# Spectral filter, real 2-D transform and MoE block: how the operands of the first group of slots reach TensorE

## The chip, the cores and the metric

One core of a Trainium2 chip runs the whole kernel. The metric is device time in microseconds (us), the median of several executions of the program. Before the change it is 1440.38 us.

## The reference

```python
def _attn_ref(x, filt_r, filt_i):            # x: 8 x 3136 x 256
    X = np.fft.rfft(x, axis=1)
    F = (filt_r + 1j * filt_i)[None, :, :]
    Y = X * F
    return np.fft.irfft(Y, n=x.shape[1], axis=1).astype(np.float32)

def _moe_ref(x, w_ch1, w_ch2):               # x is the result of _attn_ref
    X = np.fft.fft(x, axis=1)
    X = np.fft.fft(X, axis=2)
    mixed = np.real(X).astype(np.float32)
    u = x + mixed
    mu = np.mean(u, axis=-1, keepdims=True)
    var = np.mean((u - mu) ** 2, axis=-1, keepdims=True)
    un = (u - mu) / np.sqrt(var + 1e-06)
    ch = np.maximum(un @ w_ch1, 0.0) @ w_ch2
    return (u + ch).astype(np.float32)
```

So each batch is filtered in the frequency domain along its 3136 positions, the real part of a 2-D transform of the result is added, and a layer norm with a two-layer network (256 to 1024 to 256) follows, whose output is added to u.

## The kernel before, in words

**Work.** The transform of length 3136 = 56 x 56 is done in two stages of matmuls, forward and back. For each batch: `forward1` makes the first stage (matmul `s`, copies `ast`) and stores it to DRAM (`d1`), `forward2` loads it turned (`at`), makes the second stage, multiplies with the filter (`yt`), folds the spectrum into `ef` and `eo` for the mixing and transposes it to `z`, `inverse1` makes the first inverse stage (matmul `i`, copies `bt`, DRAM `d2`), and `inverse2` loads that (`b`), makes the second (`y`), and stores it slot by slot (`ys`, DRAM `dy`). A slot is a pair of positions (n and 3136 - n), 1568 of them to a batch. The second half works on 49 groups of 256 slots, in two tiles of 128: `mixture` makes the transform along channels from the folded spectrum (matmul `mix`, a row `nyq` for the middle frequency), `add` adds it to y on VectorE (DVE), `moments` and `scales` make the layer norm's numbers, `prepare` makes un, its two float16 halves `u16` and their transpose `ut` (by a transposing DMA), `first_product` makes eight `h` (6 matmuls of 512 columns each; relu on ScalarE (ACT), low half on DVE), `second_product` makes `acc` (96 matmuls of 256 columns a group), which is added to y and stored.

**Group 0** is a case of its own, since it ends the run-up: its y is made by `direct` (L776) for tile 0 and 1 from `b_0` and `b_1`, two loads of 512 KB from the DRAM copy `d_f` that the 14 stores of L699 filled; its mixture is copied (`near` L1001, `point` L1002) and added with eight operations on DVE and four of one row (L924); its `ut` is transposed on TensorE (PE; L313), not by a DMA. `prepare_first` holds this.

**Weights** come as pairs of words, are widened (L1147 to L1154), squared for a bound (L1158), bounded (L1197, L1199, a power of two through a matmul `pb` and L296 to L303) and split in a high and a low half (ACT L1223, DVE L1210): first `w1`, then `w2` between group 0's first products. Tables at L49 to L55 (LOAD_AT, WIDEN_AT, SQUARE_AT, BOUND_AT, SPLIT_AT) say at which step. **Warm** matmuls (L283, `idle`, result unused) stand on PE where it would wait in the run-up: 18 behind `inverse1`, 10 behind the mixture, 4 behind each of six pairs of y.

**Order.** A generator for each batch and the loop over q (group and eighth of it) near L1343 place the work; a scheduler moves instructions within each engine, held by `with after(...)` marks. Group 1 and on need only batch 0 until group 6, the first that needs batch 1. Batch 1's `forward1` starts behind group 0's end, and batch 2's while group 5 runs. Each engine runs its own instructions in order, DMAs of SP (SyncE) too.

Of the kernel before, what the change touches and what calls it, by code (L numbers as in the profile page):

```python
# [49 lines left out]
LOAD_AT = (2, 2, 2, 2, 41, 42, 46, 50)  # L50
LOAD_IN = ("b2", "b2", "ys", "ys", "b2", "b2", "ys", "ys")
WIDEN_AT = (31, 33, 37, 41, 58.3, 58.3, 74, 74)
SQUARE_AT = (44, 46, 58.1, 58.1, 68, 68, 1002, 1002)
BOUND_AT = (58.2, 1003)
# [38 lines left out]
def constants():  # L93
# [83 lines left out]
    cols = np.arange(56)  # L177
    near = np.zeros((112, 2, 128))
    far = np.zeros((112, 2, 256))
    for kind in range(2):  # L180
        s_, q = cols // 28, cols % 28
        near[:, kind, :56] = i2f[0].reshape(112, 112)[:, 56 * s_ + 28 * kind + q]
        far[:, kind, 112:168] = i2f[1].reshape(112, 112)[:, 56 * (s_ if kind == 0 else 1 - s_) + 28 * kind + q]
    direct = np.concatenate([near.reshape(112, 256), far.reshape(112, 512)], 1)
# [16 lines left out]
        "c_y": np.ascontiguousarray(direct).astype(np.float32),  # L201
# [14 lines left out]
def _program(ctx, tc, nc, a, NB):  # L216
# [91 lines left out]
    def flip(dst, src, pool, tag, name, late):  # L308

        m, n, q = src.shape  # L310
        pt = pool.tile([128, 8, 128], F16, tag=tag, name=name)
        for i in range(n):
            nc.tensor.transpose(pt[:q, i, :m], src[:, i], ident16[:m, :m])  # L313
# [16 lines left out]
    def settle():  # L330
# [5 lines left out]
        homes["y16"] = [*y16s, cp.tile([128, 4, 2, 128], F16, name="y16_3")]  # L336

    sxs, alphas, dys, esps = {}, {}, {}, {}

# [9 lines left out]
    def prepare_filters():  # L349
# [4 lines left out]
        pow2(mF[:, 11:12], "F", pF, spare)  # L354
# [12 lines left out]
    def first_forward1():  # L367
# [23 lines left out]
        load_weights(3)  # L391
# [5 lines left out]
        tables["y"] = direct[:112]  # L397
        nc.sync.dma_start(direct, a["c_y"])
# [44 lines left out]
    def forward1(b, d1):  # L443
# [3 lines left out]
        for q in range(7 + XLAG):  # L447
            with after(("y", 1), ("un", 0)) if b == 1 and q > 2 else after(("b", 1)) if b == 1 else nullcontext():
# [3 lines left out]
                k = q - XLAG  # L452
                if k >= 0 and b in SQUARED:
# [55 lines left out]
    def load_halves():  # L509
# [4 lines left out]
        with after("sp"):  # L514
            nc.sync.dma_start(s1, a["c_s1"])
            fill_tails(0, 1)
# [10 lines left out]
    def forward2(b, d1, d2):  # L527
# [25 lines left out]
        def spectrum(ch, hf):  # L553
# [57 lines left out]
            if b == 0:  # L611
# [3 lines left out]
                for j in range(4):  # L615
                    nc.tensor.transpose(pt[:, j], yh[:, :, j].rearrange("p r q -> p (r q)"), ident)
# [16 lines left out]
        def fold_sums(ch):  # L633
            yt = yts[ch]
            pool, tag, bufs = (fp, "ef", 1) if b else (mp, "u16", 2) if ch < 2 else (fp, "x16", 3)
# [19 lines left out]
        def fold_halves(ch):  # L655
# [6 lines left out]
            for r0, e0, n in ((g0, 0, cut), (0, cut, 224 - cut)):  # L662
                if n:
# [6 lines left out]
                    else:  # L670
                        with after("spread", "utt", "w2s", ("cast", 1)):
                            nc.scalar.activation(hi, e, AF.Copy, scale=first)
# [3 lines left out]
        def inverse1(ch, h):  # L676
# [4 lines left out]
            if b == 0:  # L681
# [4 lines left out]
                if j == 26:  # L686
                    idle.append(ps_o.tile([128, 512], F32, tag="pso", name="idle"))
                    warm(18, "i1", ("pb", "F"), p=idle[0])
                marks["spread"] = nc.scalar.copy(bt, p).ins
            else:  # L690
# [7 lines left out]
                nc.vector.tensor_tensor(bt[:, :, 1], p, bt[:, :, 0], op=ALU.subtract)  # L698
            marks["bt", ch] = nc.sync.dma_start(d2[:112, j : j + 2], bt).ins  # L699

        far = 3
        for c in range(far if b else 0):
            load(c)
            yield
        ups = {(0, 0): 1, (0, 1): 2, (1, 0): 3, (1, 1): 4, (3, 0): 5, (4, 0): 6}
# [27 lines left out]
    def inverse2(b, d2):  # L733
# [29 lines left out]
        def direct(t, tile0, tile1):  # L763

            p = bank(f"y0_{t}").rearrange("p (k c) -> p k c", k=2)
            table = tables["y"]
            for k in range(2):
                first, last = (0, 2) if t == 0 else (2, 4)
                for j in range(first, last + 1):
                    if j == 0:  # L770
                        w = table[:, 128 * k : 128 * k + 128]
                    else:
                        o = 256 + 256 * k + 112 - 56 * j + 128 * t
                        w = table[:, o : o + 128]
                    with after("warm"):
                        marks["i2"] = nc.tensor.matmul(  # L776
                            p[:, k], w, (tile0, tile1)[j // 4][:, j % 4], start=j == first, stop=j == last
# [3 lines left out]
        load(0)  # L781
        for c in range(1, 6) if b == 0 else ():
# [3 lines left out]
        for c in range(14):  # L786
            if b == 0 and c < 2:
                direct(c, bts[0], bts[1])
                if c:
                    del bts[0]  # L790
# [43 lines left out]
            with after("warm" if c < 8 else "pe"):  # L834
# [3 lines left out]
            if c < 8:  # L838
                warm(4, "i2", p=idle[0])
            with after("utt"):  # L840
# [51 lines left out]
    def fetch(g):  # L892
        y = ys_of[g] = mp.tile([128, 2, 2, 256], F32, tag="y", name=f"y_{g}", bufs=4)
        for t, (g0, g1) in enumerate(groups[g]):
            q = g0
            while q < g1:
                b = q // NS
                e = min(g1, (b + 1) * NS)
                with after(("un", 0)) if g == 2 else after(("out", g - 4)):
# [46 lines left out]
    def mixture(g):  # L946
# [4 lines left out]
        for t, (g0, g1) in enumerate(tiles):  # L951
            n = g1 - g0
            r0 = g0 % RING
            channels(pm[:n, t], lambda e, h: homes["eo"][:, e, h, r0 : r0 + n], t == 0, t == len(tiles) - 1, g == 1)
# [42 lines left out]
    def prepare_first():  # L997
# [3 lines left out]
        nc.scalar.copy(near, pm)  # L1001
        marks["near"] = nc.scalar.copy(point[:1, 0], fix[0][2]).ins  # L1002
        pm, fix = near, [(t, row, point[:1, 0], a) for t, row, _, a in fix]
        yield
        y = mp.tile([128, 2, 2, 256], F32, tag="y", name="y_0", bufs=4)
        ut = mp.tile([128, 2, 8, 128], F16, tag="ut", name="ut_0", bufs=2)
        mv, st, sb = small(0)
        al = alphas[0]
        for t in range(2):
            add(y[:, t], pm[:, t], al, sums[t])  # L1010
            for tf, row, pn, _ in fix:
                if tf == t:
                    add_nyquist(y[row, t, 1], pn, al[row], sums[t][row, 1])
            moments(0, y, [(t, groups[0][t])], st, mv)
            roots(0, sb, mv, [(128, slice(2 * t, 2 * t + 2))])
            yield
        for t in range(2):
            scales(0, sb, mv, [(128, slice(2 * t, 2 * t + 2))])
            yield
            un = mp.tile([128, 2, 256], F32, tag="un", name=f"un_0_{t}", bufs=2)  # L1020
            u16 = mp.tile([128, 2, 2, 2, 128], F16, tag="u16", name=f"u16_0_{t}", bufs=2)
            unv = un.rearrange("p k (d q) -> p k d q", q=128)
            for k in range(2):
                i = 2 * t + k
                if t and k:
                    nc.vector.tensor_scalar(un[:, k], y[:, t, k], sb[:, i, 3:4], sb[:, i, 1:2], op0=ALU.mult, op1=ALU.add)
                else:
                    nc.scalar.activation(un[:, k], y[:, t, k], AF.Identity, bias=sb[:, i, 1:2], scale=sb[:, i, 3:4])
            marks["cast", 0] = nc.scalar.copy(u16[:, :, :, 0], unv).ins
# [6 lines left out]
    def prepare(g):  # L1036
# [7 lines left out]
        for t, (g0, g1) in enumerate(tiles):  # L1044
            ps = slice(0, g1 - g0)
            with after(("u16", 0)) if g == 1 else after("h", *((("un", 1), "w2l") if g == 2 else ())):
# [36 lines left out]
    def first_product(g, f):  # L1083
# [4 lines left out]
        p = ps_h.tile([128, 512], F32, tag="psh", name=f"h_{g}_{f}")  # L1088
# [52 lines left out]
    def widen(dst, raw, name, late):  # L1141
# [12 lines left out]
        v.scalar_tensor_tensor(dst, size, tiny, dst, op0=ALU.is_ge, op1=ALU.mult)  # L1154
# [7 lines left out]
    def load_weights(i):  # L1162
# [5 lines left out]
        pool, bufs = {"b2": (fp, 2), "ys": (fp, 3)}[LOAD_IN[i]]  # L1168
# [3 lines left out]
    def widen_weights(i):  # L1172
        name = ("w1", "w2")[i // 4]
        if i % 4 == 0:
            raws[name] = [], tp.tile([128, 5], F32, tag="mw", name="m" + name)
# [5 lines left out]
        ws.append(w)  # L1181
        if a[name].dtype == F32:
            nc.sync.dma_start(w, words[i])
        else:
            with after("low", "first" if i > 4 else "", "utc"):
                widen(w, words[i], f"{i}", i > 3)

    def square_weights(i):
        name = ("w1", "w2")[i // 4]
        ws, m = raws[name]  # L1190
        with after("act", "spread" if i > 1 else "", "near" if i > 3 else "", "w1s" if i > 3 else "", "utt", "relu"):
            squares(m[:, i % 4 : i % 4 + 1], ws[i % 4], f"{name}_{i % 4}")

    def bound_weights(name):
# [3 lines left out]
        with after("utt", "relu"):  # L1198
            marks["root"] = nc.scalar.activation(m[:, 4:5], m[:, 4:5], AF.Sqrt, scale=0.25).ins  # L1199
        sw = tp.tile([128, 2], F32, tag="sw", name="s" + name)  # L1200
        pow2(m[:, 4:5], name, sw, spare, "i1" if name == "w1" else "pe")
# [236 lines left out]
```

## Time and profile before

| what | value |
|---|---|
| median of 3 runs | 1440.38 us (1440.06 to 1441.49) |
| the profiled execution | 1439.6 us, span 1437.8 us, mean granted clock 0.996 |
| PE (matmul) busy | 1394.2 us, 97% of the span |
| DVE, ACT, POOL busy | 1048.4 (73%), 755.8 (53%), 508.3 us (35%) |
| HBM read, written | 124.41 MB, 99.17 MB |

The span runs from the first to the last instruction; 1.8 us of the execution lie outside it. TensorE's matmuls take nearly all of it, so the table is read from there: the columns of the other engines matter where TensorE waits for them.

### The profile page before, as it was taken

How to read it: one execution, taken by the hardware profiler on the slowest of the kernel's cores; microseconds unless marked ns; L12 is line 12 of the kernel's file. 1: busy time of each engine (PE TensorE's matmuls, PEld its weight loads, DVE VectorE, ACT ScalarE, POOL GpSimd, SP SyncE). 2: the span in 40 equal slices, each digit the busy share in tenths (PEclk: the TensorE clock that was granted, in tenths of full speed). 3: DMA queues.
4: the chain of work that ended last, by engine and by line, in shares of the span. 5: the costliest groups of instructions: out<-in, count | busy, mean ns of one | idle time of the engine just before them, and what ended most of it. 6: DMA issues, size and time to landing. Idle time of an engine off the chain costs nothing.

```text
span 1437.8 us, 30014 instructions
## 1 busy us (share of the span) xinstructions
PE 1394.2 (97%) x11274; PEld 949.9 (66%) x11274; DVE 1048.4 (73%) x2327; ACT 755.8 (53%) x1422; POOL 508.3 (35%) x641
## 2 busy tenths in 40 slices
PE   9989999989999999999999999999999999999998
PEld 8745775557666776666766676666766667666666
DVE  7786794678688876978578866977779876555553
ACT  6757455546365554745546554655447554434341
POOL 2422591069102940067300870038401673011010
PEclk9999999999999999999999999999999999999999
DMA  9668987798947967589576987489575977453220
GB/s 358 211 210 237 240 182 238 213 209 204 257 137 205 256 159 231 157 220 240 162 229 180 245 182 224 148 222 246 139 258 167 230 179 195 112 157 78 85 60 30
DMA packets 434221, 276.42 MB, mean 192 GB/s; under 512 B 218796, under 2 KB 401084, under 8 KB 434076
## 3 DMA queue, kind: packets, MB, share of 16 engines
q1 hardware_dynamic: 433948, 274.47, 70.2%
q8 instruction: 88, 1.44, 0.4%
q14 instruction: 57, 0.47, 0.1%
q10 hardware_dynamic: 128, 0.05, 0.0%
HBM read 124.41 MB, written 99.17 MB: 155 GB/s over the span
## 4 chain that ended last, share of the span: by engine, by line
PE 63%; DVE 9%; DMA 8%; issue 5%; ACT 5%; POOL 3%; SPq 3%; DVEq 0%; ACTq 0%; POOLq 0%
PE h L1097 25%; PE acc L1127 24%; PE s L495 3%; PE y L812 2%; DMA x<-x 2%; DMA at<-d 2%; PE mix L914 2%; DVE y L924 2%; DVE h L1108 1%; ACT un L1068 1%; POOL u L1072 1%; DMA d<-ast 1%; PE s L592 1%; PE i L694 1%; PE s L593 1%
## 5 line engine op out<-in xcount | busy, mean ns | idle before, releaser
L1097 PE MATMUL h<-ut,home 128*128 128x512 f16 x2352 | 581.5, 380 | 20.9 <-DVE h L1108 12.9
L1127 PE MATMUL acc<-w2s,h 128*128 128x256 f16 x4704 | 598.5, 273 | 3.0 <-DVE y L1136 1.5
L1127 PEld LDWEIGHTS <-h 128*128 128x128 f16 x4704 | 455.1, 98 | 150.6 <-issue 17.8
L1107 ACT ACTIVATE h<-h 128x512 f16<-128x512 f32 x392 | 233.1, 595 | 390.5 <-PE h L1097 385.6
L1108 DVE SCALAR_TENSOR_TENSOR h<-h,h 128x512 f16<-128x512 f32 x392 | 267.9, 684 | 212.5 <-ACT h L1107 210.8
L1097 PEld LDWEIGHTS <-home 128*128 128x128 f16 x2352 | 222.7, 98 | 230.0 <-issue 34.3
L1072 POOL TENSOR_TENSOR u<-un,u 128x512 f16<-128x512 f32 x96 | 111.0, 1172 | 670.9 <-ACT u L1071 618.8
L924 DVE SCALAR_TENSOR_TENSOR y<-mix,alpha,y 128x508 f32<-128x508 f32 (+1 forms) x360 | 152.8, 476 | 1.7 <-PE mix L914 0.6
L1068 ACT ACTIVATE un<-y,sb 128x256 f32<-128x256 f32 x192 | 99.8, 591 | 35.3 <-DVE sb L988 33.2
L609 POOL TENSOR_TENSOR yt<-yt,t 128x224 f32<-128x224 f32 x108 | 73.4, 679 | 115.9 <-DVE t L601 87.8
L698 DVE TENSOR_TENSOR bt<-i,bt 112x512 f16<-112x512 f32 x98 | 66.4, 684 | 32.5 <-ACT bt L697 32.3
L1136 DVE SCALAR_TENSOR_TENSOR y<-acc,beta,y 128x512 f32<-128x512 f32 x98 | 71.5, 744 | 21.6 <-PE acc L1127 21.5
L821 ACT ACTIVATE ys<-y,alpha 128x512 f32<-128x512 f32 x98 | 64.1, 684 | 43.3 <-PE y L812 42.9
L639 POOL TENSOR_TENSOR ef<-yt 128x224 f32<-128x224 f32 x112 | 73.4, 675 | 34.5 <-ACT wsq_w L1158 15.7
L623 POOL TENSOR_TENSOR home<-yt,home 128x448 f16<-128x448 f32 x77 | 79.3, 1035 | 8.8 <-ACT home L622 8.8
L697 ACT CAST bt<-i 112x512 f16<-112x512 f32 x98 | 56.8, 584 | 43.0 <-PE i L696 38.3
L597 DVE SCALAR_TENSOR_TENSOR yt<-s,pF,ft 128x448 f32<-128x448 f32 x98 | 66.0, 675 | 17.4 <-PE s L593 15.5
L610 POOL TENSOR_TENSOR yt<-yt,t 128x224 f32<-128x224 f32 x108 | 74.8, 694 | 0.0
L972 DVE BATCH_NORM_STATS2 st<-y 128x6 f32<-128x256 f32 x196 | 73.1, 411 | 0.2
L306 DVE TENSOR_REDUCE mx<-x 112x1 f32<-112x1024 f32 x42 | 51.0, 1215 | 30.2 <-DMA x<-x 30.0
L601 DVE SCALAR_TENSOR_TENSOR t<-s,pF,ft 128x448 f32<-128x448 f32 x98 | 66.1, 676 | 0.5 <-POOL yt L610 0.5
L669 POOL TENSOR_TENSOR eo<-ef,eo 128x448 f16<-128x448 f32 (+6 forms) x55 | 51.5, 940 | 33.8 <-ACT eo L668 32.3
(173 smaller groups left out, 1660.8 us busy)
## 6 DMA issues: line engine op xcount, KB each, us to landing
x<-x SPq DMA_DIRECT2D x55, 512.0 KB
out<-y SPq DMA_DIRECT2D x98, 256.0 KB
at<-d SPq DMA_DIRECT2D x49, 512.0 KB
b<-d SPq DMA_DIRECT2D x49, 512.0 KB
dy<-ys SPq DMA_DIRECT2D x206, 112.0 KB
y<-dy SPq DMA_DIRECT2D x90, 256.0 KB
d<-ast SPq DMA_DIRECT2D x98, 224.0 KB
d<-bt SPq DMA_DIRECT2D x98, 224.0 KB
```

What stands on the lines that cost most here:

```text
L609: nc.gpsimd.tensor_tensor(yh[:, 0], yh[:, 0], t2v[:, 1], op=ALU.subtract)
L610: marks["sum"] = nc.gpsimd.tensor_tensor(yh[:, 1], yh[:, 1], t2v[:, 0], op=ALU.add).ins
L623: nc.gpsimd.tensor_tensor(ylo, ytv, yhi, op=ALU.subtract)
L639: nc.gpsimd.tensor_tensor(ef[:, i], yt[:, 0, i], yt[:, 1, i], op=o)
L924: nc.vector.scalar_tensor_tensor(out, p, al, y, op0=ALU.mult, op1=ALU.add)
L972: nc.vector.bn_stats(st[:m, 2 * t + k], y[:m, t, k])
L1068: nc.scalar.activation(un[:m, k], y[:m, t, k], AF.Identity, bias=sb[:m, i, 1:2], scale=sb[:m, i, 3:4])
L1072: marks["u16", g] = nc.gpsimd.tensor_tensor(u16[:m, :, :, 1], unv, u16[:m, :, :, 0], op=ALU.subtract).ins
L1097: marks["pe"] = nc.tensor.matmul(p[:, c0 : c0 + n].rearrange("p (t k q) -> p t k q", k=2, q=m), homes["w1s"][:, d, hw, 128 * f : 128 * f + ...
L1107: marks["relu"] = nc.scalar.activation(h[:, 0, :nt], p[:, :nt], AF.Relu).ins
L1108: marks["h"] = nc.vector.scalar_tensor_tensor(h[:, 1, :nt], p[:, :nt], 0.0, h[:, 0, :nt], op0=ALU.max, op1=ALU.subtract).ins
L1127: nc.tensor.matmul(acc[:m, k], h[:, hh, c0 : c0 + m], w2s[:, f, hw], start=f == 0 and k == 0 and i == 0, stop=f == 7 and k == 1 and i == 2,)
```

## The change

For batch 0 `inverse1` now also copies the 12 rows of each `bt` that group 0 needs into two tiles `near_0` and `near_1` on the chip, by 36 small DMAs on SP (16 of 1 KB rows, 20 of 2 KB rows) ahead of the stores to `d_f`; `direct` reads these tiles with two new tables (the second, 384 KB, loaded into `home`) and the load of `b_0` is gone (batch 0 still loads b from 1 on for the other slots). The mixture, scaled by alpha, is laid into y's tile ahead of y; y is then added by one operation for each tile, and roots and scales are taken once for both. w2 is bounded, widened and squared earlier or in other places; all 96 second products of group 0 stand in one piece ahead of group 1's first `h`. The warm matmuls are 8 and 2 times 6 in place of 18, 10 and 6 times 4. Cut to its core:

```diff
+def near_place(n):
+    return (n, 2) if n < 8 else ((n - 8) // 2, n % 2)
...
-LOAD_AT = (2, 2, 2, 2, 41, 42, 46, 50)
-WIDEN_AT = (31, 33, 37, 41, 58.3, 58.3, 74, 74)
+LOAD_AT = (2, 2, 2, 32, 38, 56, 57, 34)
+WIDEN_AT = (31, 33, 37, 41, 56.5, 1002, 1004, 58)
...
+        direct = home[:, 5120:6656].bitcast(F32)
+        tables["y"].append(direct)
+        nc.sync.dma_start(direct, a["c_y"][1])
...
-                if j == 26:
-                    idle.append(ps_o.tile([128, 512], F32, tag="pso", name="idle"))
-                    warm(18, "i1", ("pb", "F"), p=idle[0])
                 marks["spread"] = nc.scalar.copy(bt, p).ins
...
+            if b == 0:
+                for t in range(2):
+                    if j < 8:
+                        for i in range(2):
+                            m, blk = near_place(j + i)
+                            nc.sync.dma_start(
+                                closer[t][12 * m : 12 * m + 12, blk], bt[8 * t : 8 * t + 12, i]
+                            )
+                    else:
+                        m, _ = near_place(j)
+                        nc.sync.dma_start(closer[t][12 * m : 12 * m + 12, :2], bt[8 * t : 8 * t + 12])
             marks["bt", ch] = nc.sync.dma_start(d2[:112, j : j + 2], bt).ins
...
-        def direct(t, tile0, tile1):
+        def direct(t):
...
-                            p[:, k], w, (tile0, tile1)[j // 4][:, j % 4], start=j == first, stop=j == last
+                            p[:, k], table[:n, blk, k], closer[t][:n, blk], start=blk == 0, stop=blk == 2
...
-        load(0)
-        for c in range(1, 6) if b == 0 else ():
+        for c in range(1, 6) if b == 0 else (0,):
...
-            if c < 8:
-                warm(4, "i2", p=idle[0])
+            if c < 4:
+                warm(6, "i2", p=idle[0])
...
-        nc.scalar.copy(near, pm)
+        nc.scalar.activation(near, pm, AF.Copy, scale=al[:, 0:1])
+        nc.vector.tensor_tensor(yh[:, :, 0:4:3, 1:], even, odd, op=ALU.add)
+        nc.vector.tensor_tensor(yh[:, :, 1:3, 1:], even, odd, op=ALU.subtract)
+        nc.vector.tensor_copy(y[..., 0:129:128], near[:, :, 0:129:128].unsqueeze(2).to_broadcast([128, 2, 2, 2]))
+        for h, o in ((1, ALU.add), (0, ALU.subtract)):
+                marks["sum"] = nc.gpsimd.tensor_tensor(
+                    yh[row, t0, 2 + h, 1:], point[row, 0, 1:128], point[row, 0, 129:], op=o
+                ).ins
...
-            add(y[:, t], pm[:, t], al, sums[t])
+            nc.vector.tensor_tensor(y[:, t], sums[t], y[:, t], op=ALU.add)
...
-        p = ps_h.tile([128, 512], F32, tag="psh", name=f"h_{g}_{f}")
+        pool, tag = (ps_o, "pso") if g == 0 and f % 4 > 1 else (ps_h, "psh")
...
+    warm(8, "i1", ("pb", "F"), ("pb", "w1"), p=idle[0])
...
-            catch_up(min(q - LAG, 2 * (q - 8) + 1))
+            catch_up(8 if q == 8 else min(q - LAG, 2 * (q - 8) + 1))
...
-        if q in (4, 5):
-            split_weights("w2", 2 * q - 8)
-            split_weights("w2", 2 * q - 7)
+        if q == 7:
+            for part in range(4):
+                split_weights("w2", part)
```

VectorE between w1's low halves and group 0's layer norm, before (`home` holds w1's halves, y_0 is group 0's tile, y0_0 and y0_1 are its y in PSUM):

```order
L1210 SCALAR_TENSOR_TENSOR home_596<-w_3_600,sw1_856,home_596 128x512
L924 SCALAR_TENSOR_TENSOR y_0_925<-near_846,alpha_0_652,y0_0_911 128x4x127
L924 SCALAR_TENSOR_TENSOR y_0_925<-near_846,alpha_0_652,y0_0_911 128x4
L924 SCALAR_TENSOR_TENSOR y_0_925<-near_846,alpha_0_652,y_0_925 128x2x127 x2
L924 SCALAR_TENSOR_TENSOR y_0_925<-near_846,alpha_0_652,y0_1_918 128x4x127
L924 SCALAR_TENSOR_TENSOR y_0_925<-near_846,alpha_0_652,y0_1_918 128x4
L924 SCALAR_TENSOR_TENSOR y_0_925<-point_847,alpha_0_652,y0_0_911 1x2x127
L924 SCALAR_TENSOR_TENSOR y_0_925<-point_847,alpha_0_652,y0_0_911 1x2
L972 BN_STATS st_0_928<-y_0_925 128x6
```

And the same place now:

```order
L1242 SCALAR_TENSOR_TENSOR home_624<-w_3_627,sw1_827,home_624 128x512
L1027 TENSOR_TENSOR y_0_905<-near_901 128x2x2x127
L1028 TENSOR_TENSOR y_0_905<-near_901 128x2x2x127
L1029 COPY y_0_905<-near_901 128x8
L1186 SCALAR_TENSOR_TENSOR y16_3_625<-size_7_928,y16_3_625 128x512
L1040 TENSOR_TENSOR y_0_905<-y0_0_951,y_0_905 128x512
L989 BN_STATS st_0_967<-y_0_905 128x6 x2
L990 BN_AGGR mv_0_966<-st_0_967 128x2 x2
L1040 TENSOR_TENSOR y_0_905<-y0_1_958,y_0_905 128x512
```

What reads y's PSUM shrank to L1040, once a tile; L1027 to L1029 read only the mixture and can run before y exists.

ScalarE at the end of group 0's first products, before (L1107 is the relu that makes h16, L1223 w2's high halves, un_1 belongs to group 1):

```order
L978 ACTIVATE sb_1_1138<-mv_1_1136,eps_89 128x4
L1223 ACTIVATE w2s_93<-home_596,sw2_1256 128x2x256 x2
L1107 ACTIVATE h16_0_5_1299<-h_0_5_1292 128x512
L1223 ACTIVATE w2s_93<-home_596,sw2_1256 128x2x256
L1223 ACTIVATE w2s_93<-y16_3_597,sw2_1256 128x2x256
L1068 ACTIVATE un_1_0_1153<-y_1_1081,sb_1_1138 128x256 x2
```

And now:

```order
L1139 ACTIVATE h16_0_6_1227<-h_0_6_1220 128x512
L1139 ACTIVATE h16_0_7_1238<-h_0_7_1231 128x512
L1099 ACTIVATE un_1_0_1285<-y_1_1069,sb_1_1270 128x256 x2
L1099 ACTIVATE un_1_1_1292<-y_1_1069,sb_1_1270 128x256 x2
L1255 ACTIVATE w2s_93<-home_624,sw2_1204 128x2x256 x3
L1255 ACTIVATE w2s_93<-y16_3_625,sw2_1204 128x2x256
```

w2's high halves, ahead of the relu of h_0_5 and of group 1's un before, now stand behind the last relu of group 0 and four un; all of group 0's second products are behind them on PE.

SP's queue where batch 1 takes over, before (`d1_0<-ast_2` are batch 2's first-stage stores, `ut` groups 6 and 7, `z_2` batch 2's spectrum):

```order
L485 DMA d1_0_120<-ast_2_7_3177 112x1024
L1073 DMA_TRANSPOSE ut_6_3244<-u16_6_0_3336 128x8x128
L485 DMA d1_0_120<-ast_2_8_3224 112x1024
L485 DMA d1_0_120<-ast_2_9_3230 112x1024
L485 DMA d1_0_120<-ast_2_10_3271 112x1024
L1073 DMA_TRANSPOSE ut_6_3244<-u16_6_1_3376 128x8x128
...
L627 DMA_TRANSPOSE z_2_1_3580<-home_596 128x8x128
L536 DMA at_2_4_3716<-d1_0_120 128x8x256
L1073 DMA_TRANSPOSE ut_7_3647<-u16_7_0_3786 128x8x128
```

And now:

```order
L499 DMA d1_0_120<-ast_2_11_3272 112x1024
L499 DMA d1_0_120<-ast_2_12_3305 112x1024
L1104 DMA_TRANSPOSE ut_6_3239<-u16_6_0_3331 128x8x128
L499 DMA d1_0_120<-ast_2_13_3311 112x1024
L1104 DMA_TRANSPOSE ut_6_3239<-u16_6_1_3371 128x8x128
...
L1104 DMA_TRANSPOSE ut_7_3642<-u16_7_0_3781 128x8x128
L1104 DMA_TRANSPOSE ut_7_3642<-u16_7_1_3837 128x8x128
L640 DMA_TRANSPOSE z_2_0_3490<-home_624 128x8x128
```

Group 6's transposes moved behind four or five more stores of batch 2, group 7's moved ahead of batch 2's spectrum. DVE and POOL moved the same way: all of group 7's y and u16 now stand ahead of batch 2's `yt`.

## Rows read from the trace of the kernel before

**Rows 1.** The page's head and busy times.

```profile
span 1437.8 us, 30014 instructions
...
PE 1394.2 (97%) x11274; PEld 949.9 (66%) x11274; DVE 1048.4 (73%) x2327; ACT 755.8 (53%) x1422; POOL 508.3 (35%) x641
```

**Rows 2.** Busy us (count) of PE, PEld, DVE, ACT, POOL by stretch; PEclk, DMA share, GB/s.

```profile
80.00:130.00 50.00, 41.25 (x241) 22.67 (x240) 37.71 (x96) 37.93 (x75) 14.16 (x16) 1.00 0.63 182
90.00:110.00 20.00, 15.80 (x97) 8.55 (x95) 19.71 (x51) 13.66 (x29) 4.25 (x5) 1.00 0.75 235
310.00:320.00 10.00, 4.31 (x11) 1.59 (x12) 5.38 (x15) 1.16 (x2) 5.91 (x8) 0.66 1.15 238
```

**Rows 3.** PE's timeline, inverse stage to group 0's y: start, length, work, count, [wait].

```profile
60.52 4.05 PE L283 MATMUL idle<-still 128*128 128x512 bf16 x18
64.41 0.28 PE L914 MATMUL mix<-mix,eo 128*128 128x129 f16 x2
...
68.01 5.34 PE L776 MATMUL y<-b,direct 112*128 112x256 f32 x24
```

**Rows 4.** SP's timeline, the stores of the inverse stage and the loads behind them.

```profile
35.56 0.84 SPq L699 DMA_DIRECT2D d_f<-bt  x2
...
44.87 16.82 SPq L699 DMA_DIRECT2D d_f<-bt  x10
63.99 2.05 SPq L750 DMA_DIRECT2D b<-d_f  x4
```

**Rows 5.** SP's waits from 20 to 100 us: in total, times, longest.

```profile
SPq L699 <- ACT bt L689: 15.9, 9, 3.0
...
SPq L750 <- DMA d_f<-bt: 2.0, 1, 2.0
```

**Rows 6.** DVE's timeline, w1's low halves to group 0's low halves of un.

```profile
69.69 2.07 DVE L1210 SCALAR_TENSOR_TENSOR home<-w,sw,home 128x512 f16<-128x512 f32 x3
71.67 3.25 DVE L924 SCALAR_TENSOR_TENSOR y<-near,alpha,y 128x508 f32<-128x508 f32 x6
...
77.08 1.03 DVE L972 BATCH_NORM_STATS2 st<-y 128x6 f32<-128x256 f32 x3
...
78.62 0.36 DVE L984 RECIPROCAL sb<-sb 128x2 f32<-128x2 f32 x2 [0.29 <-ACT sb L978]
...
79.69 0.41 DVE L1026 TENSOR_SCALAR un<-y,sb 128x256 f32<-128x256 f32 x1
84.40 1.29 DVE L1030 TENSOR_TENSOR u<-un,u 128x512 f16<-128x512 f32 x2 [4.30 <-ACT u L1029]
```

**Rows 7.** PE's timeline from group 0's first product to batch 1's first stage.

```profile
87.10 1.47 PE L1097 MATMUL h<-ut,home 128*128 128x512 f16 x6 [0.79 <-DVE ut L315]
...
110.43 6.38 PE L1127 MATMUL acc<-w2s,h 128*128 128x256 f16 x57
116.88 1.46 PE L1097 MATMUL h<-ut,home 128*128 128x512 f16 x6
...
122.50 3.69 PE L481 MATMUL s<-x,s1f 112*112 112x512 f32 x8 [1.11 <-DMA s1f<-c_s1f]
```

**Rows 8.** ACT's timeline: w1's high halves, four un of group 6.

```profile
67.93 2.54 ACT L1223 ACTIVATE home<-w,sw 128x512 f16<-128x512 f32 x4
...
269.02 2.08 ACT L1068 ACTIVATE un<-y,sb 128x256 f32<-128x256 f32 x4 [1.16 <-DVE sb L988]
```

**Rows 9.** Columns of rows 2: from batch 1's first stage to group 6.

```profile
122.00:281.00 159.00, 154.07 (x1198) 99.70 (x1198) 111.36 (x235) 86.90 (x161) 63.00 (x81) 1.00 0.82 219
```

**Rows 10.** PE's timeline, first products of groups 6 and 7.

```profile
280.99 2.76 PE L1097 MATMUL h<-ut,home 128*128 128x512 f16 x12 [1.17 <-DMA ut<-u]
...
315.69 4.77 PE L1097 MATMUL h<-ut,home 128*128 128x512 f16 x12 [5.70 <-DMA ut<-u]
```

**Rows 11.** SP's timeline, group 6's second transpose.

```profile
276.90 1.40 SPq L1073 DMA_TRANSPOSE ut<-u  x1
```

**Rows 12.** POOL's timeline, the second u16 of group 7.

```profile
307.65 1.18 POOL L1072 TENSOR_TENSOR u<-un,u 128x512 f16<-128x512 f32 x1
```

More of the change, by code (lines that the diff above doesn't have):

```diff
@@ L452, in forward1 @@
                 k = q - XLAG
+                if k == 0 and b in PLAIN:
+                    table = fp.tile([112, 112], F32, tag="t2", name=f"s1f_{b}", bufs=2)
+                    nc.sync.dma_start(table, a["c_s1f"])
                 if k >= 0 and b in SQUARED:
@@ L704, in forward2 @@
             yield
+        if b == 0:
+            closer.extend(
+                fp.tile([128, 4, 256], F32, tag="ys", name=f"near_{t}", bufs=3)[:, :3] for t in range(2)
+            )
         ups = {(0, 0): 1, (0, 1): 2, (1, 0): 3, (1, 1): 4, (3, 0): 5, (4, 0): 6}
@@ L833, in inverse2 @@
             p = bank(f"y_{b}_{c}").rearrange("p (j c) -> p j c", j=2)
-            with after("warm" if c < 8 else "pe"):
+            with after("warm" if c < 4 else "turn"):
                 marks["i2"] = nc.tensor.matmul(
@@ L898, in fetch @@
                 e = min(g1, (b + 1) * NS)
-                with after(("un", 0)) if g == 2 else after(("out", g - 4)):
+                with after(("un", 0)) if g == 2 else after(("ut", 1)) if g == 3 else after(("out", g - 4)):
                     marks["y", g] = nc.sync.dma_start(
@@ L1004, in prepare_first @@
+        for h, o in ((1, ALU.add), (0, ALU.subtract)):
+            with after("sum"):
+                marks["sum"] = nc.gpsimd.tensor_tensor(
+                    yh[row, t0, 2 + h, 1:], point[row, 0, 1:128], point[row, 0, 129:], op=o
+                ).ins
+        nc.scalar.copy(y[row, t0, 1, 0:129:128], point[row, 0, 0:129:128])
         yield
-        y = mp.tile([128, 2, 2, 256], F32, tag="y", name="y_0", bufs=4)
         ut = mp.tile([128, 2, 8, 128], F16, tag="ut", name="ut_0", bufs=2)
@@ L1024, in prepare_first @@
                 i = 2 * t + k
[L1025 to L1029, printed above, removed]
+                marks["cast", 0] = nc.scalar.activation(
+                    u16[:, k, :, 0],
+                    y[:, t, k].rearrange("p (d q) -> p d q", q=128),
+                    AF.Identity,
+                    bias=sb[:, i, 1:2],
+                    scale=sb[:, i, 3:4],
+                ).ins
@@ L1184, in widen_weights @@
         else:
-            with after("low", "first" if i > 4 else "", "utc"):
+            with after("low", "utc"):
                 widen(w, words[i], f"{i}", i > 3)
@@ L1190, in square_weights @@
         ws, m = raws[name]
-        with after("act", "spread" if i > 1 else "", "near" if i > 3 else "", "w1s" if i > 3 else "", "utt", "relu"):
+        with after("act" if i < 4 else "", "spread" if i > 3 else "", "near" if i > 3 else "", "w1s" if i > 3 else "", "utt", "relu"):
             squares(m[:, i % 4 : i % 4 + 1], ws[i % 4], f"{name}_{i % 4}")
@@ L1214, in split_weights @@
         ws, sw = raws[name]
-        for i, w in enumerate(ws) if part is None else ((part, ws[part]),):
+        for i, w in sorted(ws.items()) if part is None else ((part, ws[part]),):
             if name == "w1":
@@ L1314, in _program @@
     next(first_group)
+    advance(59)
+    for ch in (2, 3, 6):
+        fold_of[0](ch)
     while come[0] < 1 + WAIT + 2:
-        weigh(63 + come[0])
-        if come[0] == 1:
-            warm(10, "mix", p=idle[0])
+        weigh(60 + come[0])
         give(come[0] + 1)
-    for i, _ in enumerate(first_group):
-        weigh(68 + i)
-        give(min(come[0] + 1, KEPT))
+    next(first_group)
+    give(come[0] + 2)
+    for _ in first_group:
+        pass
     weigh(1000)
@@ L1369, in _program @@
                 work = prepare(g + 2)
-        next(work, None)
+        if q > 7:
+            next(work, None)
         if q >= 8:
```

149 lines of the change are left out of this document (72 added, 77 removed).

## The prediction

> **What bounds the kernel now.** I read the busy times first. TensorE (PE) works for 1394.2 us of a span of 1437.8 [rows 1], 97%. So the time is TensorE's program plus the 43.6 us in which it stands still, and an edit counts only through one of three things: matmuls taken out, waits removed or added, and the clock. Next comes the table by stretch: from 80 to 130 us PE is busy 41.25 of 50 us [rows 2], which is 8.75 us of waiting while group 0 runs. DVE is busy 19.71 of the 20 us from 90 to 110, so there it sets the pace. The last row of that table, 310 to 320 us, has 5.69 us of waiting and a granted clock of 0.66. There group 7's first product waits 5.70 us for its transposed operands [rows 10], and that is the longest wait of the run-up. Before that come PE's timeline at group 0 [rows 3, 7], the same stretch of DVE and SP [rows 4 to 6], and the place where batch 1 takes over [rows 9 to 12].
>
> The profiled execution took 1439.6 us, 0.8 below the median of 1440.38. I make the sum against it and add 0.8 at the end. A measurement of this kernel tells 0.2% from no change, 2.9 us: faster is below 1437.5, slower above 1443.3.
>
> **The change part by part.**
>
> Warm matmuls. Their count falls from 18 + 10 + 24 = 52 to 8 + 12 = 20. Eighteen take 60.52 to 64.41, 0.216 each [rows 3]; 32 fewer are 6.9 us less of PE. That is worth time only if useful work moves into their place. PE's program is otherwise the same matmuls, so the span falls by 6.9 us less whatever new waiting opens.
>
> y's operands. Before, the last stores to `d_f` are issued until 61.7 (44.87 + 16.82), the first load of b at 63.99, and the direct matmuls start at 68.01 [rows 3, 4]. Now the last small copies are issued at about 62.3; the row that shows a transfer's landing here is the 2.0 us for which the load of b waited for a store [rows 5]. So y can start at 64.4, 3.6 us earlier. Its price is 36 more issues on SP. Two stores that wait for nothing else take 0.84 us to issue [rows 4], so 36 at 0.42 cost 15 us of queue. SP's queue has them free: of the 26 us from 35.56 to 61.7, 15.9 were waits for ACT's copies [rows 5]. I take no loss; the other end is in the rivals. The second table's 384 KB are loaded in the same time, beside the load of b_0 that is dropped later, and I cost them at nothing, as nothing waits for them before 64.4.
>
> Mixture in y's tile. Before, 3.25 us of DVE's six adds start at 71.67, right behind w1's low halves, and further adds, statistics and scales follow (the scales from 78.62); then DVE waits 4.30 us for ACT's high halves, and `h` starts at 87.10 [rows 6, 7]. From the end of the direct matmuls (68.01 + 5.34 = 73.3) to `h` are 13.8 us. Now come two adds (1.4, at 0.69 each like w1's low halves, three in 2.07), four statistics (1.4, three take 1.03), roots and scales (1.6, from the end of the statistics at 78.1 to the first use of the scales at 79.7), high halves straight from y (2.1: four activations of that size take 2.08 on ACT [rows 8]), and from the low halves to `h` the 2.7 us from 84.40 to 87.10: 9.2 [rows 6, 7], with two more hand-overs like the 0.29 at 78.62 about 9.8. `h` then starts at 64.4 + 5.3 + 9.8 = 79.5, 7.6 earlier. Bounds: 77 if the chain shrinks by the adds and the wait in full (3.25 and 4.30 less 1.3), 83 if the mixture is laid late behind w1's low halves and POOL's two single-row operations.
>
> w2 and the second products. Eight `h` of 6 matmuls (10.4), group 1's mixture (1.7) and five pairs of y (4.3) then take PE to 96. Behind the last relu, ACT now runs four un (2.08 for four [rows 8]) and then a high half (0.64, a quarter of 2.54 [rows 8]) and DVE a low half of 0.7. With the relu that is a **new wait of about 4 us**. The cover before was that w2 was split between first products. In exchange 96 second products run in one piece (57 take 6.45 us to the next `h` [rows 7], so 10.9 in all), and `h_1_0` comes at about 111 against 116.88. Of the 8.75 us of waiting from 80 to 130, the waits for DVE go, and the 4 us and about 3.5 smaller ones come: net -1.0, with bounds of -3 and +3.
>
> Up to batch 1's first stage. It starts at 122.5 now and at about 122.6 then, because its place in the order moved behind more of group 1: the order shows 42 second products and 18 first products that now stand ahead of it, 42 x 0.113 + 18 x 0.216 = 8.6 us [rows 3, 7]. That is 6.9 + 1.0 and some tenths. **So up to here the gain is work done ahead, not an earlier batch 1.**
>
> Handover at group 6, the first that needs batch 1. From 122 to 281 PE waits only 4.9 us [rows 9], so PE set the pace; 7.8 us less work now stands there (8.6 less group 7's mixture, 0.8, which moved in). PE would ask for group 6 at 122.6 + 157.3 - 7.8 = 272. But its operands come by batch 1's chain, which starts no earlier, and SP has the two transposes behind four and five more stores of batch 2 than before; second transpose to `h` is 4.1 us [rows 10, 11]. Bounds: 273 (wait as before, 1.17) and 281 (no gain). I take 278, since the chain speeds up where PE paced it but not on POOL, DVE and SP. Wait at group 6: 6 in place of 1.2.
>
> Group 7. Before, its u16 were formed between batch 2's spectrum work on POOL (the second at 307.65 [rows 12]) and 5.70 us of waiting followed, then 12 matmuls at half clock: 4.77 against 2.76, 2.0 us [rows 10]. Now its y, u16 and transposes stand ahead of that spectrum on DVE, POOL and SP. So 7.7 us go. Late next is batch 2's spectrum, pushed back by two u16 (1.18 each [rows 12]) and what precedes them; I put 2.5 us, bounds 0 and 5.
>
> Sum: -3.0 for group 6, -0.8 for the mixture moved ahead of it, -7.7 at group 7, +2.5 = **-9.0 us**. By the other count, 6.9 warm matmuls, 1.0 in the head, 7.7 at group 7, less 4.1 to 4.8 and 2.5: -8.3 to -9.0, the same. 1439.6 - 9.0 + 0.8 = 1431.4; I say 1431.5.
>
> **Rivals.**
>
> *The clock falls in the new gaps.* The row at 315.69 shows what 5.70 us of waiting did: twelve matmuls at the 1.2 GHz level, 2.0 us more than at 2.4 GHz [rows 10], while the waits up to 1.2 us in these rows left 1.00. The new waits of 4 (w2) and 6 us (group 6) lie near the first. Price: 2.0 to 2.5 each, so +4.5 us: 1436. The Trainium skill speaks here ("TensorE: Matmul & The Clock Gate", Why this matters for your kernels): gaps between matmul bursts should be kept short, since the engine otherwise returns to its lower clock. By that rule 32 warm matmuls fewer is a change against the clock; the trace agrees for the 5.70 us.
>
> *The handover eats it.* If batch 1's chain gives group 6 nothing before 281, and group 7 still waits 5.7 us (its u16 wait on DVE or the loads of y instead of POOL), only 0.8 is left: 1439.6. For: DMA share 0.82 and the chain's unchanged start [rows 9]. Against: group 7's move on three engines.
>
> *Larger.* Group 6 waits 1.2 as before and batch 2 loses nothing: -9.0 - 4.8 - 2.5 = -16.3, 1424; half of it 1428.
>
> *Slower: small copies hold back the inverse stage.* Each buffer of `bt` is freed when all its transfers have landed, three or five in place of one. If the 36 issues cost 0.7 us each in place of 0.42 (25 us), SP has 9 us too little in the 26 us stretch (15.9 free), and the last copy is issued at 71 rather than 62. Then y starts at 73, 5 us later than before, batch 1's inputs, behind these on SP, are late as well, and everything from 122.5 on slips 5 to 8 us: with group 7's wait still there, 1446. It decides from 9 us of delay on SP. The Trainium skill ("DMA: Bandwidth & Descriptors", Rules for kernel authors) says to join many small transfers into one, since under 64 KB one pays mostly overhead; these are 12 and 24 KB. By that rule the copies would be the cost of this change; the 2.0 us landing of a store [rows 5] speaks for a fixed cost, not for a queue that stalls.
>
> **How the numbers follow.** Forecast 0.45 (1429 to 1434); clock 0.15 (1436); larger 0.15 (1424 to 1428); handover 0.15 (1439.6); slower 0.10 (1446). Faster: 0.45 + 0.15 + 0.15 and a little of the handover, 0.78; same 0.13; slower 0.09. The range leaves out the slower case and the lowest part of the larger one: 1425 to 1441.
>
> **What would show it.** In the changed profile: `idle` 20 times; direct matmuls at 64 to 65 with no wait for a transfer; `h` at 77 to 83; one gap of 3 to 5 us ahead of the second products; batch 1's first stage near 122; group 6's `h` at 275 to 280 with a wait of 4 to 7 us; no wait over 2 us at group 7; from there on the same order, 9 us earlier. It is wrong if the direct matmuls start after 68, if batch 1's first stage starts after 126, if the clock falls behind the second products' gap, or if waits at batch 2's spectrum grow by over 5 us.

## The result and the profile after

The change makes the kernel slower: 1450.82 us (median of 4; 1450.18 to 1456.2) against 1440.22, a ratio of 1.0084 with a 95% interval of 1.0056 to 1.0112. Forecast were 1431.5 us and a range of 1425 to 1441. The profiled execution after took 1450.2 us. The lines that answer to [rows 1] and [rows 2], of the page and of the table by stretch of the changed kernel:

```profile
span 1448.3 us, 30013 instructions
...
PE 1396.3 (96%) x11242; PEld 955.5 (66%) x11242; DVE 1041.7 (72%) x2317; ACT 755.6 (52%) x1421; POOL 507.0 (35%) x643
```

```profile
80.00:130.00 50.00, 45.24 (x270) 27.41 (x269) 32.41 (x83) 34.74 (x70) 7.77 (x10) 0.96 0.85 279
90.00:110.00 20.00, 18.36 (x85) 8.33 (x82) 17.51 (x45) 15.07 (x34) 2.31 (x3) 1.00 0.72 229
200.00:250.00 50.00, 44.31 (x382) 31.85 (x381) 37.84 (x83) 25.08 (x49) 36.23 (x48) 0.90 0.74 161
134.50:305.20 170.70, 152.31 (x1156) 98.27 (x1154) 114.11 (x259) 86.76 (x161) 62.99 (x81) 0.94 0.75 200
```

32 matmuls are gone (x11242 for x11274), yet PE is busy 2.1 us longer, since more of its time lies at the 1.2 GHz level (mean granted clock 0.986, before 0.996; 0.90 from 200 to 250 us). Waiting grew from 43.6 to 52.0 us. From 80 to 130 us PE now waits 4.8 us, not 8.75, but at these times it does other work than before. Counted by its work, from group 0's first product to batch 1's first stage PE takes 41.8 us, 35.4 before, with 8.6 us of products more in it: the stretch that I had studied did improve, by some 2 us. The loss lies ahead of it and behind it. PE's timeline of the changed kernel, the answer to [rows 3, 7, 10]:

```profile
74.79 5.46 PE L796 MATMUL y<-near,direct 120*128 120x256 f32 x12 [3.99 <-DMA near<-bt]
80.04 3.12 PE L796 MATMUL y<-near,home 120*128 120x256 f32 x12
...
92.63 2.76 PE L1129 MATMUL h<-ut,home 128*128 128x512 f16 x12
...
111.56 0.58 PE L1159 MATMUL acc<-w2s,h 128*128 128x256 f16 x2 [3.20 <-ACT w2s L1255]
112.34 11.65 PE L1159 MATMUL acc<-w2s,h 128*128 128x256 f16 x94 [0.21 <-DVE w2s L1242]
123.84 1.46 PE L1129 MATMUL h<-ut,home 128*128 128x512 f16 x6
...
134.47 1.07 PE L495 MATMUL s<-x,s1f 112*112 112x512 f32 x2
...
229.82 4.99 PE L1129 MATMUL h<-ut,home 128*128 128x512 f16 x12 [1.81 <-DMA ut<-u]
...
305.19 4.85 PE L1129 MATMUL h<-ut,home 128*128 128x512 f16 x12 [4.54 <-DMA ut<-u]
```

The direct matmuls wait 3.99 us for the copies and start at 74.79, 6.8 later than before instead of 3.6 earlier, and their first half runs at half clock (5.46 for twelve, then 3.12). First products at 229.82 and 305.19 do so too, each behind a wait. Group 0's first product is 5.5 us later than before, batch 1's first stage 12.0 later, group 6 (305.19 against 280.99) 24.2 later. Group 7's wait is gone, but one of 4.54 us and the half clock behind it now stand at group 6. From there to the end 13.7 us come back, which leaves the 10.5 us of the spans. SP's timeline shows why the copies are late, an answer to [rows 4]:

```profile
35.95 3.25 SPq L714 DMA_DIRECT2D near<-bt  x4
39.25 0.51 SPq L720 DMA_DIRECT2D d_f<-bt  x1
...
72.48 1.51 SPq L719 DMA_DIRECT2D near<-bt  x2
74.04 0.51 SPq L720 DMA_DIRECT2D d_f<-bt  x1
...
76.52 5.29 SPq L775 DMA_DIRECT2D b<-d_f  x5
```

The queue runs with no wait over 0.8 us until 74.5: a copy takes SP 0.71 to 0.78 us (one 0.92), all 36 together 26.6, and a store behind them 0.40 to 0.51, where it took 0.30 to 0.45 before. The loads of b, which all other slots of batch 0 need, start at 76.5 instead of 64.0. Upstream, ACT's timeline has a `bt` copy waiting 3.04 us for its buffer:

```profile
45.96 0.59 ACT L699 COPY bt<-i 112x512 f32<-112x512 f32 x1 [3.04 <-DMA d_f<-bt]
```

### The profile page after: what moved, and what is told of

It is laid out like the page before. It is cut to its first block, busy times and chain, and to the rows that moved or that the text cites. A ratio compares the mean times of both kernels' runs of the same rounds, so it can differ in the third digit from the quotient of the medians.

```text
span 1448.3 us, 30013 instructions
## 1 busy us (share of the span) xinstructions
PE 1396.3 (96%) x11242; PEld 955.5 (66%) x11242; DVE 1041.7 (72%) x2317; ACT 755.6 (52%) x1421; POOL 507.0 (35%) x643
## 4 chain that ended last, share of the span: by engine, by line
PE 75%; DMA 8%; DVE 6%; POOL 4%; issue 3%; ACT 3%; SPq 1%; DVEq 0%; ACTq 0%; POOLq 0%
PE h L1129 29%; PE acc L1159 28%; PE s L509 3%; PE y L829 3%; PE mix L931 2%; DMA x<-x 2%; DMA d<-ast 1%; DMA at<-d 1%; PE i L704 1%; PE s L605 1%; PE i L706 1%; PE i L705 1%; PE s L606 1%; DVE y L941 1%; PE s L421 1%
```

## The experiments

**Theories.** A: the small copies hold SP, with it the inverse stage and everything behind. B: the new order costs, since batch 1's first stage stands behind more work of groups 0 and 1. C, of the rivals on record: the clock falls in waits that warm matmuls used to fill.

**The price of one transfer.** 28 transfers that nothing waits for, near the end of the kernel before.

> The kernel before with 28 extra transfers near its end that nothing waits for, to read the price of a single issue on SP: pieces of 12, 16, 20, 32, 64, 112 and 128 rows from one tile on the chip to another, and of 12 and 112 rows to DRAM, and two of 12 rows each on the queues of ACT and POOL. Theory A (the price lies in the small copies themselves): a piece of 12 rows on the chip takes SP 0.71 to 0.78 us as in the changed kernel, twice a store's 0.30 to 0.45, wherever it stands. Rival (the price came from the place: a full ring or a busy DMA system between 35 and 74 us): 12 rows take 0.30 to 0.45 here, as a store does. If A holds, the rows tell which property of a piece has the price: 12 rows against 16, or on the chip against to DRAM. The time itself is of no interest (1440 to 1447).

Measured on SP, in us: 12 rows on the chip 0.77 to 0.89 (1 KB a row) and 0.71 to 0.77 (2 KB); 20 rows 0.76; 16 rows 0.58 and 0.59; 112 rows 0.52 to 0.55; 32, 64 and 128 rows 0.49 to 0.56; 12 rows to DRAM 0.47 and 0.52, 112 to DRAM 0.46 and 0.32. In SP's timeline of this run (price_sp: on the chip, price_dram: to DRAM; the first two pairs are 12 rows):

```profile
1315.68 0.79 SPq L1389 DMA_DIRECT2D price_sp<-price_src  x1
1316.58 0.47 SPq L1391 DMA_DIRECT2D price_dram<-price_src  x1
...
1325.72 0.59 SPq L1389 DMA_DIRECT2D price_sp<-price_src  x1
```

The third line is 16 rows. So the price is the piece's own, and belongs to its kind: on the chip, and 12 or 20 rows. ACT's queue took 0.73 and 1.35, POOL 0.53 and 0.68.

**The change without its copies.** y by loads of b again, all else as changed:

```diff
-                direct(c)
+                direct(c, bts[0], bts[1])
...
-        for c in range(1, 6) if b == 0 else (0,):
+        load(0)
+        for c in range(1, 6) if b == 0 else ():
```

> The change without its small copies: y's operands come by the load of b again, all else (mixture laid into y, w2 and the second products, warm matmuls, order) as in the change. Theory A (the 36 copies hold SP, with it the inverse stage, with it everything behind): direct matmuls at 67 to 69 as before, batch 1's first stage near 125, time 1430 to 1437. Rival B (the moved second products and the order at the handover to batch 1 cost the time): 1444 to 1452, with the long waits at group 6 still there.

1447.27 us, ratio 1.0050 (1.0030 to 1.0071): only 3.5 of 10.6 us are back, and the time lies in the range of rival B. A alone has fallen. PE's timeline of this run:

```profile
69.71 7.83 PE L777 MATMUL y<-b,direct 112*128 112x256 f32 x24 [5.15 <-DMA b<-d_f]
...
106.67 13.08 PE L1143 MATMUL acc<-w2s,h 128*128 128x256 f16 x94 [0.20 <-DVE w2s L1226]
```

Where 18 + 10 warm matmuls stood, PE now has 8, waits 5.15 us and runs the direct matmuls in 7.83 us instead of 5.34 [rows 3]; the second products take 13.08. Batch 1 starts at 130.2, group 6 at 297.8.

**The copies alone**, added to the kernel before:

```diff
+                            nc.sync.dma_start(
+                                closer[t][12 * m : 12 * m + 12, blk], bt[8 * t : 8 * t + 12, i, :20]
+                            )
...
+            closer.extend(cp.tile([128, 3, 20], F32, name=f"near_{t}") for t in range(2))
```

> The kernel before with the change's 36 small copies alone (same rows and places in SP's queue, 80 bytes a row and piece because the chip's memory is full, into tiles that nobody reads). Theory A: the last store of the inverse stage is issued 8 to 12 us later than at 61.7, the direct matmuls follow, time 1446 to 1454. Rival B: within 2 us of before, since the copies are small and hidden.

1454.99 us, ratio 1.0104 (1.0082 to 1.0126): +15, the upper end of what A said. The last store is issued at 76.1 instead of 61.4, 14.7 us later where 8 to 12 were expected, and group 6 starts at 297.1. PE's timeline of this run:

```profile
82.43 7.99 PE L794 MATMUL y<-b,direct 112*128 112x256 f32 x24 [4.74 <-DMA b<-d_f]
```

A copy of 80 bytes a row cost SP 0.77 us on average, one of 1 or 2 KB in the change 0.74: bytes are not the price. Without copies the rest of the change costs 7 us (1440 to 1447), with them it gains 4 (1455 to 1451), since there the direct matmuls read the copies (from 74.8) and not what comes by `d_f` (from 82.4): the parts do not add up.

**The laid mixture alone**, in the kernel before (`prepare_first` of the change, nothing else).

> The kernel before with one part of the change: the mixture laid into y's tile, one add a tile, roots and scales once, high halves straight from y; copies, w2, warm matmuls and order as before. The chain from the direct matmuls' end to group 0's first product was 13.8 us before and 9.6 in the change. Theory (this part is sound, the loss comes from the copies and from where batch 1 stands): first product 3 to 4.5 us earlier than 87.1, batch 1's first stage and group 6 earlier by 2 to 4, time 1435 to 1438. Rival (nothing gained, since other work of DVE or ACT around 90 to 120 us sets the pace there): 1439 to 1442.

1437.25 us, ratio 0.9987 (0.9972 to 1.0001). Group 0's first product comes at 81.5, 5.6 us earlier, batch 1 at 117.8 and group 6 at 276.4, both 4.6 earlier; the span ends 2.0 us earlier. In the run-up this part does what was forecast of it, and more than half of the 4.6 us is given back further on (from 350 to 400 us PE is busy 45.67 us instead of 47.13). The interval includes 1, so a gain in time is not shown.

**Batch 1 placed as before**, without copies:

```diff
-... STEPS + 3 + 4 * (q - 6 if q > 6 else 0) if q < 14 else NB * STEPS ...
+... STEPS + 3 + 3 * (q - 3 if q > 3 else 0) if q < 16 else NB * STEPS ...
```

> The change without its copies and with the kernel before's pace for batch 1 (its steps are placed from q = 4 on by 3, not from q = 7 on by 4): PE's order then has batch 1's first stage ahead of all second products of group 0 (0 of them, 48 first products) where the change has 126 and 78 ahead. Theory (group 6 waits for batch 1's chain, which is as long as its order makes it and starts with its first stage): first stage before 115 in place of 130.2 and first stage to group 6 near 158 to 162 in place of 168, time 1428 to 1436. Rival (w2's new wait and the half clock behind it are the loss, the place of batch 1 does not matter): 1444 to 1448 as without the copies.

1454.89 us, ratio 1.0099 (1.0068 to 1.0130): a miss, and slower. PE now asks for batch 1 right behind group 0's first products, when its inputs have not arrived:

```profile
113.90 0.25 PE L303 MATMUL pb_x<-lines_x,still 112*128 112x112 bf16 x1 [11.12 <-DVE lines_x L300]
```

So too early a place costs as well; two runs further on try one between.

**28 copies of 16 rows** (a fourth block of rows, one copy for both columns of a `bt`).

> The change with 28 copies of 16 rows and 2 KB in place of 36 of 12 rows (a fourth block of rows; 16 direct matmuls in place of 12, their 4 extra cost about 1.8 us of PE in all). By the prices read at the end of the kernel before, 12 and 20 rows take SP 0.71 to 0.79 and 16 rows 0.59. Theory: 28 x 0.59 = 16.5 us of SP in place of 36 x 0.73 = 26, the last copy near 64 to 66 in place of 74, first product 5 to 8 us earlier, time 1442 to 1447. Rival (the copies' landing or bt's buffers, not SP's issues, hold the inverse stage): last copy still after 71, 1449 to 1452.

1450.81 us, ratio 1.0062 (1.0037 to 1.0087): a miss, the time of the change. SP and y did nearly as expected: 0.57 us a copy, the last ends at 67.5; the direct matmuls start at 66.73 on blocks that came before it and end at 73.9, 9 us earlier than in the change. Group 0's first product comes at 87.7, only 4.9 earlier. ACT's and DVE's timelines of this run tell why:

```profile
77.89 0.58 ACT L851 COPY ys<-y 112x512 f32<-112x512 f32 x1 [7.75 <-PE y L845]
78.38 0.30 ACT L988 ACTIVATE sb<-mv,eps 128x4 f32<-128x4 f32 x1
...
78.71 0.18 DVE L994 RECIPROCAL sb<-sb 128x4 f32<-128x4 f32 x1 [3.04 <-ACT sb L988]
```

The root of group 0's layer norm stands in ACT's queue behind a copy of the next slots' y, which needs b by way of DRAM, and DVE waits 3.04 us for it. **Group 0 was not freed of the way through DRAM.** In the change itself the same copy waits 8.89 us, but it costs nothing there: y comes so late that the root waits for its own statistics (`mv`) last.

```profile
84.12 0.58 ACT L858 COPY ys<-y 112x512 f32<-112x512 f32 x1 [8.89 <-PE y L852]
84.93 0.30 ACT L995 ACTIVATE sb<-mv,eps 128x4 f32<-128x4 f32 x1 [0.23 <-DVE mv L990]
```

With the pace of before as well:

> Both mends together: 28 copies of 16 rows, and the kernel before's pace for batch 1. Theory: the gains add up, so 5 us below the run with the pace alone if the copies now bring y early (direct matmuls by 66), the same as that run if not: 1425 to 1436. Rival (as for the pace alone): 1442 to 1447.

1454.13 us, ratio 1.0097 (1.0067 to 1.0128), a miss, with the same wait for batch 1's inputs as above (10.78 us): the mends do not add up.

**Batch 1 a little earlier** (4 a step from q = 5), without and with the copies.

> The change without its copies, batch 1's steps placed a little earlier (4 a step from q = 5 on in place of q = 6): PE's order has 73 second and 48 first products ahead of batch 1's first stage where the change has 126 and 78. With the kernel before's pace PE stood 11 us for batch 1's inputs, which were there at 113.9; here the first stage is asked for near 117, so they are there. Theory (where batch 1's first stage stands decides): first stage at 117 to 121 in place of 130.2, group 6 at 281 to 287 in place of 297.8, time 1437 to 1442. Rival (w2's wait and the half clock behind it decide): 1445 to 1448.

1444.84 us (1.0021 to 1.0052). Its first stage starts at 119.5, 10.7 us earlier, group 6 at 290.7, only 7.1 earlier, the median is 2.4 lower, and its interval overlaps that of the run without copies; 1437 to 1442 was expected. w2's wait became 6.54 us.

> The change with its 36 copies and that earlier pace (59 second and 48 first products ahead of batch 1's first stage). Theory (two costs that add up: the copies make everything 5 us later, the place of batch 1 costs about 8): 5 to 8 us above the same kernel without copies, 1442 to 1448. Rival (the place of batch 1 costs nothing): 1450 to 1452, as the change.

1451.85 us (1.0040 to 1.0089): 7.0 us above the same without copies, as expected, but no faster than the change.

**The waits filled**, without copies, place as in the change:

```diff
+        if come[0] == 1:
+            warm(24, "mix", p=idle[0])
...
             for part in range(4):
                 split_weights("w2", part)
+            warm(16, "pe", ("pb", "w2"))
```

> The change without its copies, with two waits of PE filled: 24 warm matmuls (5.2 us) behind group 0's mixture, where PE waited 5.15 us for b and then ran the direct matmuls in 7.83 us in place of 5.34, and 16 (3.5 us) ahead of the second products, where it waited 3.20 us and then took 13.1 us for 94 matmuls in place of about 10.4. Nothing else moves in PE's order. Theory (the clock that falls in the new gaps is a cost of its own in this order): direct matmuls in 5.3, second products in 10.6, first product and batch 1's first stage 2.5 and 5 us earlier, time 1441 to 1444 in place of 1447. Rival (the place of batch 1 decides, what PE does ahead of it is hidden): 1446 to 1448.

1438.54 us, ratio 0.9993 (0.9982 to 1.0004): 8.7 us below the run without them, more than expected. PE's timeline of this run:

```profile
64.08 5.34 PE L287 MATMUL idle<-still 128*128 128x512 bf16 x24
...
103.73 10.42 PE L1143 MATMUL acc<-w2s,h 128*128 128x256 f16 x94 [0.32 <-DVE w2s L1226]
```

The direct matmuls take 5.3 us, the second products 10.42; batch 1 starts 5.2 and group 6 4.9 us earlier. 40 matmuls whose result nobody uses, put into waits, pay for themselves: **C is the loss without copies.** With the earlier place besides, and 14 fillers more ahead of the second products (30, some 3.0 us), since the wait there grows:

> The change without its copies, with the waits filled (24 and 30 warm matmuls) and batch 1's first stage placed earlier (85 second and 48 first products ahead of it, 126 and 78 in the change). Theory (place and clock are two costs and both are mended): first stage at 116 to 119 in place of 125.0, group 6 at 284 to 288 in place of 292.9, time 1433 to 1437. Rival (the place no longer matters once the clock holds): 1437 to 1440, as with the waits filled alone.

1438.15 us (0.9975 to 1.0013): no different. Batch 1 at 116.7 and group 6 at 282.4, 8 and 10.5 us earlier, move the end by nothing that the runs show. **B, as far as it is the place of batch 1's first stage, is no cost that these runs show.** The rest of the change's order was not undone in any run.

**The waits filled in the change itself**, copies and all:

> The change itself, whole and with its 36 copies, with 18 warm matmuls behind group 0's mixture (it waited 3.99 us for the copies there and ran the first 12 direct matmuls in 5.46 us, the next 12 in 3.12) and 16 ahead of the second products (wait 3.20, then 11.65 for 94). Theory (the clock's part adds to the copies' part): direct matmuls 2.3 us and second products 1.2 us shorter, batch 1's first stage 3 to 4 us earlier, time 1442 to 1447, the rest to before being the copies'. Rival (with the copies as the late part, the clock is hidden): 1449 to 1452.

1450.47 us (1.0051 to 1.0088): nothing. The direct matmuls run at full clock (24 in 5.4 us), PE waits next for b of the other slots, and now the root of group 0 does wait for the copy of their y:

```profile
74.68 2.76 PE L796 MATMUL y<-near,direct 120*128 120x256 f32 x12
...
82.67 1.86 PE L852 MATMUL y<-b,i2f 112*112 112x512 f32 x2 [2.64 <-DMA b<-d_f]
...
85.39 0.18 DVE L1001 RECIPROCAL sb<-sb 128x4 f32<-128x4 f32 x1 [3.62 <-ACT sb L995]
```

**What beats both.** The laid mixture in the kernel before, 8 warm matmuls fewer and batch 1's table loaded earlier:

```diff
-            if c < 8:
+            if c < 6:
                 warm(4, "i2", p=idle[0])
```

> The kernel before with the laid mixture, and two small parts more: the warm matmuls behind the last two pairs of y are gone (8 of 52; with the laid mixture they stand between group 0's first products, 1.7 us), and the table of batch 1's first stage is loaded earlier, as in the change (its wait was 1.08 us). Theory (PE sets the pace in this stretch now): batch 1's first stage at 115 to 116 in place of 117.8, time 1433 to 1437. Rival (DVE, or the next batches' starts, take it back): 1437 to 1439, as with the laid mixture alone.

1434.72 us, ratio 0.9962 (0.9940 to 0.9983). Group 6 starts at 272.6 in the profiled execution, which was the fastest of ten (1428.44). These 8 warm matmuls stood between products whose operands were there. How much of the gain comes from each of the three parts is not shown: the interval overlaps that of the laid mixture alone.

## Why the prediction was wrong

| kernel | direct | first product | batch 1 | group 6 | median |
|---|---|---|---|---|---|
| before | 68.0 | 87.1 | 122.5 | 281.0 | 1440.2 |
| change | 74.8 | 92.6 | 134.5 | 305.2 | 1450.8 |
| change, waits filled | 74.7 | 94.0 | 134.6 | 303.0 | 1450.5 |
| without copies | 69.7 | 87.0 | 130.2 | 297.8 | 1447.3 |
| without copies, waits filled | 69.3 | 84.0 | 125.0 | 292.9 | 1438.5 |
| laid mixture alone | 67.5 | 81.5 | 117.8 | 276.4 | 1437.3 |

- **y's operands: the step that failed first.** It costed 36 issues at 0.42 us, the row of a store, 15 us, and took no loss. A copy on the chip of 12 rows takes 0.71 to 0.78, 26.6 us in all, so the direct matmuls start at 74.8 and not at 64.4. The rival "small copies hold back the inverse stage" had the mechanism and the price (0.7 us, last copy at 71, 1446); it had a chance of 0.10, and left group 7's wait in place, which went. The Trainium skill ("DMA: Bandwidth & Descriptors", Rules for kernel authors) advises joining many small transfers; the runs agree in direction, but what they show as the price is SP's issue, and 16 rows instead of 12 lower it.
- **Nothing queued behind was costed.** The loads of b stand behind the copies on SP (76.5), and a copy of y that needs them stands ahead of group 0's root on ACT. That costs nothing in the change, but as soon as y comes earlier DVE waits for the root: 3.04 us with copies of 16 rows, 3.62 with the waits filled. The prediction moved group 0's y alone.
- **Warm matmuls, -6.9: wrong as a gain.** PE has 32 fewer and is busy 2.1 us longer. The clock rival priced a fall at 2.0 to 2.5 us for each wait; filled, the two waits of the run without copies were worth 8.7. Of this 2.5 and 2.7 us are the matmuls behind them and 4.9 are seen at group 6; where the rest arises behind it no run shows. The rule of the Trainium skill that was cited ("TensorE: Matmul & The Clock Gate", Why this matters for your kernels) holds here: 5.15 us of waiting, then 7.83 for 5.34.
- **Laid mixture: right.** From the direct matmuls' end to the first product 9.8 us were forecast and 9.6 measured (83.0 to 92.6).
- **w2: right in place, the clock left out.** A wait of 4 us was forecast, 3.20 came; the 96 second products took 12.3 to the next first product, not 10.9, and 13.7 without the copies.
- **Batch 1's start and group 6.** 122.6 was forecast and 134.5 came, since the first product is 13 us late against the forecast. From there to group 6 I took 155 us and wrote that the chain speeds up; it took 170.7, against 158.5 before. 4.1 of this were to be read from the order: 14 second and 12 first products more stand between the first stage's own matmuls (28.1 us long instead of 24.0). Moving work ahead left only more waiting here: 18.4 us (last line of the table by stretch), 4.9 before [rows 9]. That is what the rival "the handover eats it" was about, and no fault of the copies: without them and with the waits filled the stretch takes 167.9 us and group 6 still waits 5.17. (In the orders shown five and three more stores stand ahead of group 6's transposes, not four and five.) But the two runs with the waits filled and two places of batch 1 show that lateness at group 6 is mostly given back behind it, and the end follows it only in part.
- **Group 7: right in place.** Its wait of 5.70 us and the half clock behind it are gone, but at group 6 a wait of 4.54 us (6 was forecast) brings the half clock (4.85 us for twelve), which the forecast left out; from group 6 to the end 13.7 us are saved, forecast 6.

Undoing the copies alone gives 3.5 us, filling the waits alone nothing, both 12.3: two causes in a row, each hiding the other. With both undone the time is that of before (ratio 0.9993), so nothing of the forecast 9 us is left even then. What stays open is why not, and why the laid mixture's 4.6 us shrink to some 2 at the later batches; no run here shows it.

## What to carry to other kernels

Before adding transfers to a queue, measure the issue of that very kind once, at an idle end of the kernel; a row of another kind can be half of it. When an operand comes earlier, follow each engine's queue from it to the result and look for instructions ahead that still need the old way. Count filler matmuls as cover: taking them out of a wait brings back the wait and the clock behind it; eight taken from between ready products cost nothing here.

## What the runs showed of the hardware

On SP the issue of a copy on the chip depended on its rows, not its bytes: 12 and 20 rows 0.71 to 0.92 us, 16 rows near the end of the kernel 0.58 and 0.59, 112 rows 0.52 to 0.55, 32, 64 and 128 rows 0.49 to 0.56, and 12 rows to DRAM 0.47 to 0.52; 80 bytes a row cost as much as 2 KB.
